# Gate weights rewritten with one-input VectorE operations, adapter casts moved to ScalarE, and the stages put in a new order, in a fused RWKV6 attention and adapter-mixture kernel

## The chip, the cores and the metric

The kernel runs on one core of a Trainium2 chip. The metric is device time in microseconds (us), the median of several executions. Each execution is called fast or slow by its time against the fastest of the same kernel, and only fast runs enter a ratio. The engines are TensorE (PE in the profile, with its weight loads as PEld), VectorE (DVE), ScalarE (ACT), GpSimd (POOL) and SyncE (SP, which here only issues transfers). In these traces each engine takes its instructions in the order in which the program gives them (GpSimd stands 16.1 us at one cast, below), and the kernel fixes that order by hand. SBUF and PSUM are the two memories in which the kernel keeps its tiles: TensorE's products go to PSUM, and nearly everything else lies in SBUF.

## The reference

Two computations follow each other. The first is a recurrence with a decay for each channel (4 batches, 8 heads, 768 steps, 48 channels a head), the second a mixture of low-rank adapters on its output (3072 rows of 384, 8 adapters of rank 16, the best two for each row):

```python
for t in range(S):                                   # S = 768
    cur = einsum('bhd,bhe->bhde', u[None] * kt, vt)
    y[:, :, t] = einsum('bhd,bhde->bhe', rt, state + cur)
    state = wt[:, :, :, None] * state + einsum('bhd,bhe->bhde', kt, vt)
# x = y, laid out as 3072 rows of 384
logits = x @ w_gate                                  # 8 adapters
topk = the two largest of each row;  w = softmax over these two
out = x + sum over the two of w * (x @ A[e]) @ B[e]
```

## The kernel before

The recurrence is cut into 24 tiles of 128 time steps (6 for each batch). For every tile the kernel multiplies r and k by exponentials of summed logarithms of the decay, takes products on TensorE under a triangular mask, and adds what comes from the state. The step's own term, (sum of r·k·u)·v, is made separately: GpSimd multiplies r·k and then by u, VectorE reduces (`diag`), and GpSimd multiplies v by the result. The gate of the mixture is worked out once for four tiles (at the end for two).

Every stage is a function of the tile number t. It has an offset, and the sorted values of t + offset are the program order. An offset therefore decides what stands before what on every engine.

```python
BATCHES = (4, 4, 4, 4, 4, 2, 2)
OFFSET = dict(load=-12.000, ln=-4.318, rk1=-4.189, rku=-4.068, cs=-2.895, exps=-2.541,
    vcast=-2.385, diag=-2.133, dv=-1.717, mult=-2.159,
    # ... cut ...
    lgmm=1.897, adapters=-6.500, gate=2.015, gate2=2.055, zmm=2.129, zw=2.332, zT=2.344,
    zTev=2.602, dmm=2.746, oev=2.790, store=2.913)

def mult(t):          # VectorE: the "r,k product", 128 x 768, two inputs from SBUF
    nc.vector.tensor_mul(rk2[...], st[t]["rk"][...], st[t]["e2"][...])

def rk1(t):           # GpSimd
    rku_ = wk.tile([L, H, D], F32, name="rku")            # two buffers
    nc.gpsimd.tensor_mul(rku_, st[t]["rk"][:, 0], st[t]["rk"][:, 1])
def rku(t):
    nc.gpsimd.tensor_mul(st[t]["rku"], st[t]["rku"], u_sb)
def diag(t):          # VectorE; frees the buffer rku and releases dv
    nc.vector.tensor_reduce(out=dg, in_=st[t]["rku"], axis=AX.X, op=ALU.add)
def dv(t):            # GpSimd
    nc.gpsimd.tensor_mul(dv_, st[t]["v"], st[t]["diag"].to_broadcast([L, H, D]))

def gate2(t):         # VectorE, n = 4 tiles at once; E = 8
    for i in range(n):
        nc.vector.max(out=top[:, i, :], in_=ge[:, i, :])
    nc.vector.tensor_tensor(out=sel, in0=ge, in1=top[:, :, 1:2].to_broadcast([L, n, E]), op=ALU.is_ge)
    nc.vector.tensor_add(den, top[:, :, 0:1], top[:, :, 1:2])
    nc.vector.reciprocal(out=den, in_=den)
    nc.vector.tensor_mul(sel, sel, ge)
    nc.vector.tensor_mul(g, sel, den.to_broadcast([L, n, E]))
# zmm: TensorE x @ A, in the PSUM buffer tagged "m".  zw: VectorE, z times g ("the weighting").
# zT, zTev: transposed, in "m" again.

D_TAG = {NT - 2: "y_ps", NT - 1: "a_ps"}
def dmm(t):           # TensorE: x + zw @ B, in "m" except for the last two tiles
    d_ps = pp.tile([L, HD], F32, name="d_ps", tag=D_TAG.get(t, "m"))
    # ... cut ...

def adapters(t):      # once, at offset -6.5: behind the early loads, ahead of rk1(0)
    nc.sync.dma_start(out=wg_sb, in_=...)     # and A, in three parts, and B
    nc.gpsimd.tensor_copy(out=wg_bf, in_=wg_sb)
    nc.gpsimd.tensor_copy(out=Aall, in_=Aall_f...)
    nc.gpsimd.tensor_copy(out=Ball, in_=Ball_f)
```

The softmax here doesn't subtract the row's maximum and nothing guards it: scores larger than these inputs give would overflow.

## Time and profile before

The time is 141.54 us (median of four runs, 140.98 to 143.12). The end of VectorE's r,k product is a good milestone, because every tile has one and VectorE is close to full in the middle. The trace gives these:

| milestone, us | before |
|---|---|
| second r,k product ends | 27.04 |
| eighth r,k product ends (the start) | 49.22 |
| then four rounds of four tiles, each with one gate | 17.21, 17.76, 17.78, 17.20 |
| last (24th) r,k product ends | 119.17 |
| from there to the end of the span (the tail) | 20.53 |

The first view is the page of before. After the busy times of the engines come rows of 40 digits. Each digit is the busy share, in tenths, of a fortieth of the span; PEclk is the clock that TensorE was granted. The last line is a group of instructions: operation, count, busy time and mean, then the idle time before it and what ended that.

```profile
span 139.7 us, 3124 instructions
PE 90.2 (65%) x1204; PEld 62.6 (45%) x1204; DVE 104.0 (74%) x177; ACT 88.6 (63%) x161; POOL 82.7 (59%) x91
...
DVE  6120000489999999999999999999999899987220
...
POOL 7000005999999996899907999169991597200000
PEclk9999999999999995999999999959998699986755
...
L416 POOL CAST wg_bf<-wg_sb 128x24 bf16<-128x24 f32 x1 | 0.2, 204 | 16.1 <-DMA wg_sb<-in_moe_w_gate_dram 16.1
```

VectorE's row is 9 from slice 10 to slice 35, but for one 8, so VectorE limits the middle. It is nearly empty before, and so is GpSimd's row. The group says what GpSimd does in that time: it waits 16.1 us for the gate weights, which it is to cast.

The second view is that of the waits: who waited, for what, total us, times, longest.

```profile
DVE diag L244 <- POOL rku L240: 17.1, 2, 16.2
...
POOL wg_bf L416 <- DMA wg_sb<-in_moe_w_gate_dram: 16.1, 1, 16.1
...
POOL rku L236 <- DVE diag L244: 14.6, 4, 4.3
```

VectorE stands 16.2 us for the first r·k·u product, which stands behind the casts in GpSimd's program. The third line is another matter: four times GpSimd is out of work for up to 4.3 us, until a `diag` frees a buffer. The next two views show one such place, first VectorE's timeline (start, duration, line, operation).

```profile
64.88 1.55 DVE L223 TENSOR_TENSOR rk_3_150<-rk_in,e_1019 128x768 bf16<-128x768 f32 x1
66.35 0.54 DVE L244 TENSOR_REDUCE diag<-rku 128x8 f32<-128x384 f32 x1
66.81 0.36 DVE L350 MAX8 top<-ge 128x8 f32<-128x8 f32 x4
67.20 0.92 DVE L352 TENSOR_TENSOR sel<-ge,top 128x32 f32<-128x32 f32 x1
...
68.33 0.87 DVE L356 TENSOR_TENSOR sel<-sel,ge 128x32 f32<-128x32 f32 x1
69.23 0.75 DVE L358 TENSOR_TENSOR g<-sel,den 128x32 f32<-128x32 f32 x1
70.09 0.69 DVE L373 TENSOR_TENSOR zw<-z_ps,g 128x512 bf16<-128x512 f32 x1
```

Here is GpSimd's timeline at the same time. The bracket holds the idle time before an instruction and what ended it.

```profile
67.08 1.00 POOL L236 TENSOR_TENSOR rku<-rk_in 128x384 f32<-128x384 f32 x1
68.16 1.00 POOL L240 TENSOR_TENSOR rku<-rku,u_sb 128x384 f32<-128x384 f32 x1
69.11 0.83 POOL L249 TENSOR_TENSOR dv<-v_in,diag 128x384 f32<-128x384 f32 x1
74.23 1.00 POOL L236 TENSOR_TENSOR rku<-rk_in 128x384 f32<-128x384 f32 x1 [4.30 <-DVE diag L244]
```

Read the two together. `diag` ends just before the gate begins and gives GpSimd three products to run, from 67.08 to 69.94. Nearly all of VectorE's gate falls on these. Three operations have 32 elements and take 0.92, 0.87 and 0.75 us, each ending near the end of a GpSimd product. In before's last full gate, where GpSimd has run out of work, the last two take 0.16 and 0.19 us. The gate takes 3.28 us from its maxima to the weighting (66.81 to 70.09), and then GpSimd has nothing to do for 4.3 us. In this trace the two engines hold each other up: VectorE's r,k product takes 0.95 us alone and 1.55 us beside GpSimd (64.88), and the GpSimd product beside it (`dv`, 65.57) takes 1.54 us in place of 0.83.

The last view is that of windows, for the tail: the stretch, its length, busy time and count of PE, PEld, DVE, ACT and POOL, then granted TensorE clock (1.00 is full), DMA share and GB/s.

```profile
119.17:139.70 20.53, 12.16 (x129) 7.76 (x128) 9.94 (x36) 6.86 (x16) 0.83 (x1) 0.71 0.24 87
```

No engine is full there.

### The profile page before, as it was taken

What the parts mean: (1) busy time and instruction counts of PE and PEld (TensorE: products, weight loads), DVE (VectorE), ACT (ScalarE), POOL (GpSimd) and SP (SyncE); (2) the same over time, 40 slices, a digit from 0 to 9 for tenths busy, and PEclk for the clock granted to TensorE, in tenths of its full rate; (3) what the DMA queues carried; (4) which work ended last, traced back from release to release, by engine and by line L of the source; (5) the groups of instructions that cost most, each with busy time, mean ns of one, the idle gap of its engine ahead of it and who ended that gap; (6) DMA issues with size and microseconds to landing.
All of it is one profiled execution on the core that took longest, in us unless ns stands there. A gap on an engine that the chain in (4) does not pass through costs nothing. (4 is left out here: it accounts for less than half of the span.)

```text
span 139.7 us, 3124 instructions
## 1 busy us (share of the span) xinstructions
PE 90.2 (65%) x1204; PEld 62.6 (45%) x1204; DVE 104.0 (74%) x177; ACT 88.6 (63%) x161; POOL 82.7 (59%) x91
## 2 busy tenths in 40 slices
PE   1362400297776928997559784599864997777570
PEld 0131100254555714774547563386653775656320
DVE  6120000489999999999999999999999899987220
ACT  4045600098798962899939998279992799622521
POOL 7000005999999996899907999169991597200000
PEclk9999999999999995999999999959998699986755
DMA  4799999999999300897918811011110111111314
GB/s 145 183 349 391 342 83 300 380 392 387 382 387 386 132 0 2 191 299 252 347 48 281 280 63 56 0 61 56 61 56 0 56 58 62 61 56 56 113 56 169
DMA packets 17470, 24.39 MB, mean 175 GB/s; under 512 B 4912, under 2 KB 14384, under 8 KB 17456
## 3 DMA queue, kind: packets, MB, share of 16 engines
q1 hardware_dynamic: 17456, 24.20, 52.0%
q8 instruction: 9, 0.15, 0.4%
q14 instruction: 5, 0.04, 0.1%
HBM read 19.48 MB, written 4.72 MB: 173 GB/s over the span
## 5 line engine op out<-in xcount | busy, mean ns | idle before, releaser
L236 POOL TENSOR_TENSOR rku<-rk_in 128x384 f32<-128x384 f32 x24 | 27.5, 1146 | 14.6 <-DVE diag L244 14.6
L263 ACT COPY rkT<-trp 128x1024 bf16<-128x1024 bf16 x24 | 24.8, 1032 | 17.1 <-PE trp L257 17.1
L249 POOL TENSOR_TENSOR dv<-v_in,diag 128x384 f32<-128x384 f32 x24 | 28.5, 1188 | 2.0 <-DVE diag L244 2.0
L278 DVE TENSOR_TENSOR at<-a_ps,at_mask 128x1024 bf16<-128x1024 f32 x24 | 29.1, 1214 | 0.0
L244 DVE TENSOR_REDUCE diag<-rku 128x8 f32<-128x384 f32 x24 | 13.0, 543 | 17.9 <-POOL rku L240 17.1
L240 POOL TENSOR_TENSOR rku<-rku,u_sb 128x384 f32<-128x384 f32 x24 | 24.6, 1024 | 1.9
L404 ACT COPY res<-d_ps 128x384 f32<-128x384 f32 x24 | 12.0, 501 | 19.9 <-PE d_ps L399 15.2
L315 DVE TENSOR_TENSOR xs<-dv,y_ps 128x384 bf16<-128x384 f32 x24 | 13.1, 544 | 1.5 <-PE y_ps L309 1.3
L327 ACT COPY xT<-xT_ps 128x384 bf16<-128x384 bf16 x24 | 12.4, 515 | 2.5 <-PE xT_ps L322 2.4
L231 ACT CAST v_bf<-v_in 128x384 bf16<-128x384 f32 x24 | 13.1, 545 | 0.0
L257 PE MATMUL trp<-ident,rk_1_146 128*128 128x128 bf16 x48 | 4.1, 235 | 12.8 <-DVE rk_1_146 L223 12.7
L200 ACT ACTIVATE logw<-w_in 128x768 f16<-128x768 f32 x11 | 9.4, 855 | 3.5 <-DMA w_in<-in_w_dram 3.5
L383 PE MATMUL zT_ps<-ident,zw 128*128 128x128 bf16 x24 | 2.9, 243 | 12.9 <-DVE zw L373 12.9
L398 PE MATMUL d_ps<-xs,ident 128*128 128x384 bf16 x24 | 8.9, 371 | 3.4 <-DVE zT L390 2.6
L212 PE MATMUL cs_ps<-logw,co_strict 128*128 128x384 f16 x20 | 7.3, 367 | 5.8 <-ACT e_197 L218 3.3
L272 PE MATMUL a_ps<-rkT 48*128 48x128 bf16 x192 | 10.6, 236 | 0.0
L294 ACT CAST S_sb<-s_ps 128x384 bf16<-128x384 f32 x20 | 10.3, 513 | 0.0
L214 PE MATMUL cs_ps<-logw,strict 128*128 128x384 f16 x24 | 8.9, 372 | 1.6 <-ACT logw L197 1.6
L416 POOL CAST wg_bf<-wg_sb 128x24 bf16<-128x24 f32 x1 | 0.2, 204 | 16.1 <-DMA wg_sb<-in_moe_w_gate_dram 16.1
L309 PE MATMUL y_ps<-v_bf,at 128*128 128x48 bf16 x192 | 9.4, 189 | 0.5 <-DVE at L278 0.5
L322 PE MATMUL xT_ps<-ident,xs 128*128 128x128 bf16 x72 | 8.6, 232 | 1.5 <-ACT rkT L263 1.4
L257 PEld LDWEIGHTS <-rk_1_146 128*128 128x128 bf16 x48 | 3.1, 105 | 13.7 <-DVE rk_1_146 L223 13.3
(124 smaller groups left out, 219.9 us busy)
## 6 DMA issues: line engine op xcount, KB each, us to landing
rk_in<-in_rk_dram SPq DMA_DIRECT2D x24, 384.0 KB, 6.6
v_in<-in_v_dram SPq DMA_DIRECT2D x24, 192.0 KB, 6.1
out_dram<-res SPq DMA_DIRECT2D x24, 192.0 KB, 1.9
w_in<-in_w_dram SPq DMA_DIRECT2D x11, 384.0 KB, 6.5
w_in<-in_w_dram SPq DMA_DIRECT2D x2, 192.0 KB, 3.5
u_sb<-in_u_dram SPq DMA_DIRECT2D x1, 192.0 KB, 6.7
Aall_f<-in_moe_A_dram SPq DMA_DIRECT2D x3, 64.0 KB, 4.9
Ball_f<-in_moe_B_dram SPq DMA_DIRECT2D x1, 192.0 KB, 3.7
```

The costliest lines, as they stand in the source:

```text
L231: nc.scalar.copy(out=v_bf, in_=st[t]["v"])
L236: nc.gpsimd.tensor_mul(rku_.rearrange("p h d -> p (h d)"), st[t]["rk"][:, 0], st[t]["rk"][:, 1])
L240: nc.gpsimd.tensor_mul(st[t]["rku"], st[t]["rku"], u_sb)
L244: nc.vector.tensor_reduce(out=dg, in_=st[t]["rku"], axis=AX.X, op=ALU.add)
L249: nc.gpsimd.tensor_mul(dv_, st[t]["v"], st[t]["diag"].to_broadcast([L, H, D]))
L263: nc.scalar.copy(out=rkT, in_=st[t]["trp"])
L272: nc.tensor.matmul(a_ps[:, g, p, :], lhsT=rkT[base:base + D, 1, p, :], rhs=rkT[base:base + D, 0, p, :], start=True, stop=True)
L278: nc.vector.tensor_mul(at, st[t]["a_ps"].rearrange("s g p f -> s (g p) f"), at_mask.to_broadcast([128, H, 128]))
L294: nc.scalar.copy(out=sb, in_=S_acc)
L315: nc.vector.tensor_add(xs, st[t]["dv"].rearrange("p a b -> p (a b)"), st[t]["y_ps"].rearrange("p a b -> p (a b)"))
L327: nc.scalar.copy(out=xT_, in_=st[t]["xT_ps"])
L404: nc.scalar.copy(out=res, in_=st[t]["d_ps"])
```

## The change

The change has four parts. The gate loses its three 32-element two-input operations on VectorE; four `tensor_scalar` (compare, then multiply, with two scalars for each row) and a reduction come in, and GpSimd makes one last 32-element product. The adapter casts go to ScalarE, in the middle of its work. The loads go out in another order. And nearly all offsets are new. The intent is to free the start from the late adapter loads and to keep the gate out of GpSimd's way.

```diff
-    load=-12.000,
+    load_w=-14.300,  load_rk=-12.200,  load_v=-12.100,      (was one stage; u now before v)
-    rk1=-4.189,  rku=-4.068,  diag=-2.133,  dv=-1.717,  mult=-2.159,
+    rk1=-2.324,  rku=-2.092,  diag=-0.953,  dv=-0.189,  mult=-2.543,
-    lgmm=1.897,  gate=2.015,  gate2=2.055,  zmm=2.129,  zw=2.332,
+    lgmm=1.556,  gate=1.745,  gmax=1.849,  gsel=1.921,  zmm=2.027,  zw=2.052,
+    casts=1.179,
     ... the other offsets also change; cut, several of them put on one line here ...

-        nc.vector.tensor_tensor(out=sel, in0=ge, in1=top[:, :, 1:2].to_broadcast([L, n, E]), op=ALU.is_ge)
-        nc.vector.tensor_add(den, top[:, :, 0:1], top[:, :, 1:2])
+        nc.vector.tensor_reduce(out=den, in_=top[:, :, 0:2], axis=AX.X, op=ALU.add)
         nc.vector.reciprocal(out=den, in_=den)
-        nc.vector.tensor_mul(sel, sel, ge)
-        nc.vector.tensor_mul(g, sel, den.to_broadcast([L, n, E]))
+        for i in range(n):
+            nc.vector.tensor_scalar(out=sel[:, i, :], in0=ge[:, i, :], scalar1=top[:, i, 1:2],
+                                    scalar2=den[:, i, :], op0=ALU.is_ge, op1=ALU.mult)
+    def gsel(t):
+        nc.gpsimd.tensor_mul(g, st[t]["sel"], st[t]["ge"])

     def adapters(t):
         ...
-        nc.gpsimd.tensor_copy(out=wg_bf, in_=wg_sb)
-        nc.gpsimd.tensor_copy(out=Aall, in_=Aall_f.rearrange("p a e r -> p a (e r)"))
-        nc.gpsimd.tensor_copy(out=Ball, in_=Ball_f)
+    def casts(t):
+        nc.scalar.copy(out=wg_bf, in_=wg_sb)
+        nc.scalar.copy(out=Aall, in_=Aall_f.rearrange("p a e r -> p a (e r)"))
+        nc.scalar.copy(out=Ball, in_=Ball_f)
```

More of the change, by code (lines that the diff above doesn't have):

```diff
@@ L22 @@
 BATCHES = (4, 4, 4, 4, 4, 2, 2)
-STAGES = ("load", "ln", "cs", "exps", "mult", "vcast", "rk1", "rku", "diag", "dv", "tr", "trev", "amm", "aev",
-          "kv", "sev", "ymm", "xev", "xT", "xTev", "lgmm", "adapters", "gate", "gate2", "zmm", "zw", "zT", "zTev",
+STAGES = ("load_w", "load_rk", "load_v", "ln", "ln1", "cs", "exps", "mult", "vcast", "rk1", "rku", "diag", "dv", "tr", "trev", "amm", "aev",
+          "kv", "sev", "ymm", "xev", "xT", "xTev", "lgmm", "adapters", "casts", "gate", "gmax", "gsel", "zmm", "zw", "zT", "zTev",
           "dmm", "oev", "store")
 OFFSET = dict(
-    load=-12.000,
-    ln=-4.318,
-    rk1=-4.189,
-    rku=-4.068,
-    cs=-2.895,
-    exps=-2.541,
-    vcast=-2.385,
-    diag=-2.133,
-    dv=-1.717,
-    mult=-2.159,
-    tr=-1.719,
-    trev=-1.349,
-    amm=-0.767,
-    aev=-0.334,
-    kv=-1.651,
-    sev=-0.667,
-    ymm=0.203,
-    xev=0.439,
-    xT=1.112,
-    xTev=1.398,
-    lgmm=1.897,
-    adapters=-6.500,
-    gate=2.015,
-    gate2=2.055,
-    zmm=2.129,
-    zw=2.332,
-    zT=2.344,
-    zTev=2.602,
-    dmm=2.746,
-    oev=2.790,
-    store=2.913,
+    load_w=-14.300,
+    load_rk=-12.200,
+    load_v=-12.100,
+    ln=-4.517,
+    ln1=-3.548,
+    rk1=-2.324,
+    rku=-2.092,
+    cs=-3.307,
+    exps=-2.892,
+    vcast=-2.132,
+    diag=-0.953,
+    dv=-0.189,
+    mult=-2.543,
+    tr=-1.890,
+    trev=-1.762,
+    amm=-0.918,
+    aev=-0.628,
+    kv=-1.628,
+    sev=-0.979,
+    ymm=-0.097,
+    xev=0.063,
+    xT=0.823,
+    xTev=0.891,
+    lgmm=1.556,
+    adapters=-6.500,
+    casts=1.179,
+    gate=1.745,
+    gmax=1.849,
+    gsel=1.921,
+    zmm=2.027,
+    zw=2.052,
+    zT=2.119,
+    zTev=2.310,
+    dmm=2.544,
+    oev=2.763,
+    store=2.994,
 )
@@ L78, in plan @@
         for t in range(NTILE):
-            if f in ("gate", "gate2", "zmm", "zw", "zT", "zTev") and t not in gate_at:
+            if f in ("gate", "gmax", "gsel", "zmm", "zw", "zT", "zTev") and t not in gate_at:
                 continue
@@ L82, in plan @@
                 continue
-            if f == "adapters" and t > 0 or f == "ln" and t > 0 and t % 2:
+            if f in ("adapters", "casts") and t > 0 or f in ("ln", "ln1", "load_w") and t % 2:
+                continue
+            if f.startswith("load") and t == 0 or f == "ln1" and t > 0:
                 continue
@@ L125, with load_w, load_rk, load_v @@
     st = {t: {} for t in range(NT)}
-    def load(t):
-        if t % 2 == 0:
-            w_in = io.tile([L, 2, HD], F32, name="w_in", bufs=(AHEAD + 4) // 2)
-            if t == 0:
-                nc.sync.dma_start(out=w_in[:, 0], in_=w[0])
-            else:
-                nc.sync.dma_start(out=w_in, in_=w[t:t + 2].rearrange("c p f -> p c f"))
-            st[t]["w"] = w_in
-            st[t + 1]["w"] = w_in
+    def load_w(t):
+        w_in = io.tile([L, 2, HD], F32, name="w_in", bufs=(AHEAD + 4) // 2)
+        for i in range(2):
+            st[t + i]["w"] = w_in
+        if t == 0:
+            for i in range(2):
+                nc.sync.dma_start(out=w_in[:, i], in_=w[i])
+        else:
+            nc.sync.dma_start(out=w_in, in_=w[t:t + 2].rearrange("c p f -> p c f"))
+    def load_rk(t):
         rk_in = io.tile([L, 2, HD], F32, name="rk_in")
         nc.sync.dma_start(out=rk_in, in_=rk[t])
+        st[t]["rk"] = rk_in
+    def load_v(t):
         v_in = io.tile([L, H, D], F32, name="v_in")
         nc.sync.dma_start(out=v_in.rearrange("p h d -> p (h d)"), in_=v[t])
-        st[t].update(rk=rk_in, v=v_in)
-        if t == 0:
-            nc.sync.dma_start(out=st[0]["w"][:, 1], in_=w[1])
+        st[t]["v"] = v_in
+    u_sb = const.tile([128, H, D], F32)
+    def load_u(t):
+        nc.sync.dma_start(out=u_sb, in_=u.partition_broadcast(128))
     gate_at, _ = batches()
     GMAX = max(BATCHES)
-    order = plan()
-    n_pre = next(i for i, (f, _) in enumerate(order) if f != "load")
-    load(0)
-    u_sb = const.tile([128, H, D], F32)
-    nc.sync.dma_start(out=u_sb, in_=u.partition_broadcast(128))
-    for _, t in order[1:n_pre]:
-        load(t)
+    load_w(0)
+    load_rk(0)
+    load_u(0)
+    load_v(0)
     ident = const.tile([128, 128], BF16)
@@ L197, in ln, with ln1 @@
             nc.scalar.activation(out=logw[:, 0], in_=st[0]["w"][:, 0], func=ACT.Ln)
-            nc.scalar.activation(out=logw[:, 1], in_=st[0]["w"][:, 1], func=ACT.Ln)
         else:
             nc.scalar.activation(out=logw, in_=st[t]["w"], func=ACT.Ln)
-        st[t]["logw"] = logw[:, 0]
-        st[t + 1]["logw"] = logw[:, 1]
+        for i in range(2):
+            st[t + i]["logw"] = logw[:, i]
+    def ln1(t):
+        nc.scalar.activation(out=st[1]["logw"], in_=st[1]["w"][:, 1], func=ACT.Ln)
     def cs(t):
@@ L340, in gate, with gmax @@
         st[t]["ge"] = ge
-    def gate2(t):
+    def gmax(t):
         t0, n = gate_at[t]
         ge = st[t]["ge"]
-        def small(nm, w_):
-            return wk.tile([L, GMAX, w_], F32, name=nm)[:, 0:n, :]
-        top = small("top", E)
+        top = wk.tile([L, GMAX, E], F32, name="top")[:, 0:n, :]
+        den = wk.tile([L, GMAX, 1], F32, name="den")[:, 0:n, :]
+        sel = wk.tile([L, GMAX, E], F32, name="sel")[:, 0:n, :]
         for i in range(n):
             nc.vector.max(out=top[:, i, :], in_=ge[:, i, :])
-        sel = small("sel", E)
-        nc.vector.tensor_tensor(out=sel, in0=ge, in1=top[:, :, 1:2].to_broadcast([L, n, E]), op=ALU.is_ge)
-        den = small("den", 1)
-        nc.vector.tensor_add(den, top[:, :, 0:1], top[:, :, 1:2])
+        nc.vector.tensor_reduce(out=den, in_=top[:, :, 0:2], axis=AX.X, op=ALU.add)
         nc.vector.reciprocal(out=den, in_=den)
-        nc.vector.tensor_mul(sel, sel, ge)
-        g = small("g", E)
-        nc.vector.tensor_mul(g, sel, den.to_broadcast([L, n, E]))
+        for i in range(n):
+            nc.vector.tensor_scalar(out=sel[:, i, :], in0=ge[:, i, :], scalar1=top[:, i, 1:2],
+                                    scalar2=den[:, i, :], op0=ALU.is_ge, op1=ALU.mult)
+        st[t]["sel"] = sel
+    def gsel(t):
+        t0, n = gate_at[t]
+        g = wk.tile([L, GMAX, E], F32, name="g")[:, 0:n, :]
+        nc.gpsimd.tensor_mul(g, st[t]["sel"], st[t]["ge"])
         st[t]["g"] = g
@@ L413, in adapters @@
             nc.sync.dma_start(out=Aall_f[:, j, :, :],
-                                in_=moe_A[:, j * 128:(j + 1) * 128, :].rearrange("e fi r -> fi e r"))
+                              in_=moe_A[:, j * 128:(j + 1) * 128, :].rearrange("e fi r -> fi e r"))
         nc.sync.dma_start(out=Ball_f, in_=moe_B.rearrange("e r d -> (e r) d"))
-        nc.gpsimd.tensor_copy(out=wg_bf, in_=wg_sb)
-        nc.gpsimd.tensor_copy(out=Aall, in_=Aall_f.rearrange("p a e r -> p a (e r)"))
-        nc.gpsimd.tensor_copy(out=Ball, in_=Ball_f)
-    fns = dict(load=load, ln=ln, cs=cs, exps=exps, mult=mult, vcast=vcast, rk1=rk1, rku=rku, diag=diag, dv=dv, tr=tr,
+    def casts(t):
+        nc.scalar.copy(out=wg_bf, in_=wg_sb)
+        nc.scalar.copy(out=Aall, in_=Aall_f.rearrange("p a e r -> p a (e r)"))
+        nc.scalar.copy(out=Ball, in_=Ball_f)
+    fns = dict(load_w=load_w, load_rk=load_rk, load_v=load_v, ln=ln, ln1=ln1, cs=cs, exps=exps, mult=mult, vcast=vcast, rk1=rk1, rku=rku, diag=diag, dv=dv, tr=tr,
                trev=trev, amm=amm, aev=aev, kv=kv, sev=sev, ymm=ymm, xev=xev, xT=xT, xTev=xTev, lgmm=lgmm,
-               adapters=adapters, gate=gate, gate2=gate2, zmm=zmm, zw=zw, zT=zT, zTev=zTev, dmm=dmm, oev=oev,
+               adapters=adapters, casts=casts, gate=gate, gmax=gmax, gsel=gsel, zmm=zmm, zw=zw, zT=zT, zTev=zTev, dmm=dmm, oev=oev,
                store=store)
     with tc.manual_schedule(engines={ENG.PE, ENG.Activation, ENG.DVE, ENG.Pool, ENG.SP}):
-        for f, t in order[n_pre:]:
+        for f, t in plan():
             fns[f](t)
```

## The prediction

> **What bounds the kernel now.** Three stretches.
>
> 1. Start, 0 to 27 us. By the timeline, GpSimd has its masks by 3.3 us and then stands until 19.4 at the cast of the gate weights (page, groups: 16.1 us idle, released by its DMA, behind 17 loads in the queue). The casts of A and B follow to 23.2. Behind them, in order, are the r*k*u products; VectorE waits 16.2 us for the first (view of waits), so its second r,k-times-exp product ends only at 27.0.
> 2. Middle. VectorE is 97% busy (windows, 40 to 100). A tile without a gate takes 3.54 us: GpSimd's three products (1.07 + 0.96 + 0.78) plus 0.72 in which VectorE's r,k-times-exp product shuts them out. That product takes 0.95 us alone, 1.56 beside GpSimd; GpSimd's first product then 1.71 instead of 0.99. [...] With a gate in every fourth, four tiles take 17.77 us (72.74 to 90.51). There, three 128x32 two-input operations cost 0.92, 0.87 and 0.75 us beside GpSimd; the last two take 0.16 and 0.19 in the last full gate, without it. GpSimd then idles 4.3 us.
> 3. Tail, from the last r,k product (ends 119.2) to 139.7: gates, TensorE, ScalarE, stores in turn; GpSimd is done.
>
> **What changes.**
> - Casts leave GpSimd: its products can begin when tile 0's r,k land, near 6 us. I estimate the second r,k product near 13 us instead of 27.0 (tile 1's loads near 11, by the pace of before's loads). Given back: ScalarE does the casts after its fifth Exp, near 20 us, but the adapters' DMAs (4.4 us of issue, 83 GB/s) land near 22 to 24, one 384 KB load later than before; ScalarE stands 2 to 3 us. Net at the eighth tile: -12.9 us (49.2 to 36.3).
> - Gate: out go the three two-input operations; in come one reduction (0.15) and four tensor_scalar of 8 elements [...]; GpSimd gets one 32-element product [...]. [...] But the order leaves GpSimd little to run then, so I expect one block of at most 1 us per gate. No trace yet shows it.
> - rku no longer follows rk1 directly, saving 0.12 us: GpSimd-bound tiles near 3.4.
> - Four tiles then take about 15.6 us (estimate: VectorE sum 13.8, plus 1.8 of exclusion and waits; ScalarE 14.0). Four rounds: -8.7 us.
> - Tail: unchanged within 1 us.
>
> **Prediction.** 141.5 - 12.9 - 8.7 = 119.9 us; range 115.5 to 124. Faster by over 2%: 0.97; within 2%: 0.02; slower: 0.01.
>
> **What would show each step.** GpSimd's r*k products from about 6 us, no 16 us wait; second r,k product near 13; a ScalarE wait of 2 to 3 us on an adapter DMA; rounds of 15.6 us, no 4.3 us GpSimd idle (under 1.5)[...].
>
> **What would make it wrong.** Each tensor_scalar blocked by a GpSimd product (+2 us per gate, 128 us in all); tile 1's loads later than 11 us; the ScalarE stand longer; ScalarE (3.5 us per tile) or a slowed TensorE clock becoming the limit; or better sharing (15.0 per round, 117).

The sum came to 119.9 us (141.5 − 12.9 − 8.7). After's trace has 0.195 us from one `tensor_scalar` to the next, 0.287 us in the record of one, and 0.25 us for GpSimd's product of 32 elements. The cut figure of `tensor_scalar` is inside VectorE's 13.8 us of a round. In before's trace the rest of that sum is about 13.4 us, an estimate from the starts of VectorE's instructions: four times the 2.93 us of the tile from 72.74 to 75.67, and 1.7 for what is left of the gate from 84.58 to 89.38. So about 0.4 us of it stood for the four `tensor_scalar`. The other parts are near numbers of the same trace: ScalarE is busy for 14.18 us from 72.74 to 90.51 (14.0 in the prediction), three r,k products beside GpSimd lose three times 0.61 us (1.8), and the addition that the reduction replaces takes 0.153 us (0.15).

## The result, and the profile after

The time after is 123.03 us (median of four, 122.42 to 123.49), against 141.54 in the same rounds. The ratio is 0.872, with a 95% interval of 0.865 to 0.879. A ratio here is the record's own figure for the fast runs of the same rounds, so it is not quite the ratio of the medians quoted. The medians are of all runs, and some hold a slow one (e1, e5, e7 and e8 one each, e2 two, and before in the two later sets of rounds); the profiles read are of fast runs unless the text says otherwise. Before's own median was 141.3 to 141.9 us in the later comparisons. After itself was not run again there.

| us | before | after | difference | predicted |
|---|---|---|---|---|
| eighth r,k product ends | 49.22 | 35.08 | −14.1 | −12.9 |
| eighth to last | 69.95 | 63.37 | −6.6 | −8.7 |
| last to end of span | 20.53 | 22.75 | +2.2 | 0 (within 1) |
| span | 139.7 | 121.2 | −18.5 | −21.6 |

Each of these is read from one profile. After, e7 and e11 below have the same program up to the tail, and their eighth product ends at 35.08, 35.19 and 36.60 us, so a single difference of 1 us is not to be leaned on. After's rounds are 15.67, 15.67, 16.35 and 15.68 us. The page of after has these rows:

```profile
span 121.2 us, 3161 instructions
PE 88.6 (73%) x1204; PEld 62.1 (51%) x1204; DVE 97.8 (81%) x180; ACT 89.9 (74%) x164; POOL 81.5 (67%) x95
...
DVE  6350799866999999999999999999999999862200
...
POOL 7045999986588599965999658696969973200000
PEclk9999999985999999999999967999999997555555
```

GpSimd works from the third slice on and VectorE, at 6 tenths or more until the tail, from the fifth. In the last seven slices the clock is at 5 in six. The waits of after:

```profile
POOL g L375 <- DVE sel L368: 11.1, 6, 5.2
...
POOL rku L250 <- DVE diag L258: 9.5, 7, 1.4
...
POOL rku L250 <- DMA rk_in<-in_rk_dram: 5.3, 2, 4.0
```

The 16 us wait for the gate weights is gone; what GpSimd waits for first is tile 0's own r and k, for 4.0 us. The wait for `diag` is 1.4 us at most, where it was 4.3. The largest wait, for the gate's `sel`, holds mostly time in the tail, where GpSimd has little else to do (5.2 us the longest). ScalarE's timeline shows the casts in their new place:

```profile
21.20 0.22 ACT L435 CAST wg_bf<-wg_sb 128x24 bf16<-128x24 f32 x1
21.76 0.51 ACT L436 CAST Aall<-Aall_f 128x384 bf16<-128x384 f32 x1 [0.33 <-DMA Aall_f<-in_moe_A_dram]
22.77 0.51 ACT L437 CAST Ball<-Ball_f 128x384 bf16<-128x384 f32 x1 [0.51 <-DMA Ball_f<-in_moe_B_dram]
```

ScalarE stands 0.33 + 0.51 = 0.84 us for the transfers. Next are the timelines at a gate, of VectorE and then of GpSimd:

```profile
64.98 1.44 DVE L237 TENSOR_TENSOR rk_3_126<-rk_in,e_1348 128x768 bf16<-128x768 f32 x1
66.34 0.36 DVE L364 MAX8 top<-ge 128x8 f32<-128x8 f32 x4
66.74 0.16 DVE L365 TENSOR_REDUCE den<-top 128x4 f32<-128x8 f32 x1
...
67.15 0.87 DVE L368 TENSOR_SCALAR sel<-ge,top,den 128x8 f32<-128x8 f32 x4
67.93 0.54 DVE L258 TENSOR_REDUCE diag<-rku 128x8 f32<-128x384 f32 x1
68.45 0.69 DVE L390 TENSOR_TENSOR zw<-z_ps,g 128x512 bf16<-128x512 f32 x1
```

```profile
65.56 1.72 POOL L254 TENSOR_TENSOR rku<-rku,u_sb 128x384 f32<-128x384 f32 x1
68.17 0.25 POOL L375 TENSOR_TENSOR g<-sel,ge 128x32 f32<-128x32 f32 x1 [0.88 <-DVE sel L368]
68.55 1.00 POOL L250 TENSOR_TENSOR rku<-rk_in 128x384 f32<-128x384 f32 x1
```

From the maxima to the weighting now takes 2.11 us (66.34 to 68.45), and a `diag` is in it. But note what GpSimd does from 67.29 to 68.17: nothing. It ran out of work 0.13 us after the start of the first `tensor_scalar`: next in its order is the gate's own product `g`, which needs the results of all four, and behind that a product whose buffer the `diag` after the fourth sets free. So the trace of after cannot say whether these operations escape GpSimd, or whether GpSimd was simply not there. In the tail the window of after reads:

```profile
98.45:121.20 22.75, 12.50 (x101) 7.37 (x97) 10.68 (x35) 6.16 (x14) 3.20 (x6) 0.57 0.20 73
```

The clock is 0.57 against 0.71, and the tail is 2.2 us longer. VectorE's timeline shows where the time goes in, counted from the last r,k product: the last product under the mask starts at 6.17 us (5.87 in before), the last gate's maxima at 12.69 (11.79), the last weighting at 15.39 (13.65). So the delay grows step by step, 0.3, 0.9, 1.7 and at the end 2.2 us. Just before that weighting VectorE waits 1.56 us for TensorE's z product, where before it waited 0.86.

### The profile page after: what moved, and what is told of

Its sections match the earlier page's. It is cut to its first block, busy times and chain, and to the rows that moved or that the text cites. A ratio compares the mean times of both kernels' runs of the same rounds, so it can differ in the third digit from the quotient of the medians.

```text
span 121.2 us, 3161 instructions
## 1 busy us (share of the span) xinstructions
PE 88.6 (73%) x1204; PEld 62.1 (51%) x1204; DVE 97.8 (81%) x180; ACT 89.9 (74%) x164; POOL 81.5 (67%) x95
## 4 chain that ended last, share of the span: by engine, by line
DVE 33%; DMA 22%; ACT 15%; PE 13%; issue 9%; SPq 5%; DVEq 0%; ACTq 0%; POOLq 0%
DMA v_in<-in_v_dram 15%; DVE at L292 6%; DVE rk_3_126 L237 5%; DMA rk_in<-in_rk_dram 4%; ACT rkT L277 4%; SPq L430 3%; DVE diag L258 3%; DVE sel L368 3%; DVE xs L329 3%; ACT res L421 3%; DVE rk_2_124 L237 3%; PE d_ps L415 3%; DVE zw L390 3%; DMA Ball_f<-in_moe_B_dram 2%; PE d_ps L416 2%
## 5 line engine op out<-in xcount | busy, mean ns | idle before, releaser
L254 POOL TENSOR_TENSOR rku<-rku,u_sb 128x384 f32<-128x384 f32 x24 | 35.6, 1485 | 0.5 <-DMA u_sb<-in_u_dram 0.5
L250 POOL TENSOR_TENSOR rku<-rk_in 128x384 f32<-128x384 f32 x24 | 23.9, 996 | 15.4 <-DVE diag L258 9.5
L263 POOL TENSOR_TENSOR dv<-v_in,diag 128x384 f32<-128x384 f32 x24 | 19.9, 827 | 2.5 <-DVE diag L258 2.4
L336 PEld LDWEIGHTS <-xs 128*128 128x128 bf16 x72 | 6.3, 104 | 7.1 <-issue 4.9
L375 POOL TENSOR_TENSOR g<-sel,ge 128x32 f32<-128x32 f32 (+1 forms) x7 | 1.7, 242 | 12.0 <-DVE sel L368 11.1
L416 PE MATMUL d_ps<-Ball,zT 128*128 128x384 bf16 x24 | 9.4, 392 | 0.0
L228 PE MATMUL cs_ps<-logw,n_incl 128*128 128x384 f16 x24 | 8.8, 368 | 0.0
```

Source lines behind the costliest of these rows:

```text
L228: nc.tensor.matmul(o, lhsT=wb, rhs=lw, start=False, stop=True, skip_group_check=True)
L250: nc.gpsimd.tensor_mul(rku_.rearrange("p h d -> p (h d)"), st[t]["rk"][:, 0], st[t]["rk"][:, 1])
L336: nc.tensor.transpose(xT_ps[:, j, :], st[t]["xs"][:, j * 128:(j + 1) * 128], ident)
```

## The experiments

Twelve kernels ran, and all gave correct results. The questions were these. Is the start a matter of the casts alone? Is the gain of the middle due to the new gate operations (the theory of the prediction) or to the gate's new place ahead of `diag` (the rival)? And where do the 2.2 us of the tail come from?

### Casts alone, gate operations alone, both

`e1_casts` is before with the casts on ScalarE, behind the fifth exponential:

```diff
+    casts=1.465,
-        nc.gpsimd.tensor_copy(out=wg_bf, in_=wg_sb)       (and the two others)
+    def casts(t):
+        nc.scalar.copy(out=wg_bf, in_=wg_sb)              (and the two others)
```

> The kernel before, with one part of the change: the three adapter casts go from GpSimd to ScalarE, after its fifth Exp, as in the changed kernel. Theory 'queue order': GpSimd's products stood only behind the casts, so they begin near 7 us, the second r,k product ends near 13 to 14 us instead of 27.0, rounds of four tiles stay near 17.5 us, and the time is 128 to 130 us. Rival 'loads': tile 1 is held by its own loads or by TensorE, so less than half of that comes, 135 us or more.

Measured: 130.31 us against 141.9 (ratio 0.919, 0.911 to 0.927), just above the 128 to 130 expected. The second r,k product ends at 13.97 and the eighth at 34.5, both within 1 us of after's. The casts alone are therefore worth 11.6 us of the time. At the eighth tile they bring 14.7 us, but the middle then takes 71.9 us in place of 69.95, and the tail 21.53 in place of 20.53, which gives 2.9 of it back. Its rounds are 17.39 to 18.46 us; why the middle became longer was not tested.

`e2_gate` is before with only the gate's operations replaced, in the old place:

```diff
-    gate2=2.055,
+    gmax=2.055,
+    gsel=2.056,       (with gmax and gsel as in the kernel after)
```

> The kernel before, with only the gate's new operations (reduction, four tensor_scalar, product on GpSimd), at the old place in the order, where GpSimd is busy. Theory 'no blocking': the four tensor_scalar take about 0.9 us as in the changed kernel, each 0.28 to 0.29 us in the record, each gate saves 1 to 1.5 us, time 134 to 137 us. Rival [...]: tensor_scalar is shut out by GpSimd's products too; single ones take up to 1 us, four take over 1.5 us, and the time is 138 us or more.

Measured: 144.85 us, ratio 1.010 (1.001 to 1.020): no gain, at most a small loss. Its profiled run was a slow one, so no reading of its trace is used here. Two of its four runs were slow ones too; the ratio uses the other two (143.1 and 144.35).

`e3_casts_gate` is the two together.

```diff
  e1_casts, and:
-    gate2=2.055,
+    gmax=2.055,
+    gsel=2.056,
```

> The kernel before with both parts, casts and gate operations, but the old order of stages and loads. What is left to the changed kernel (123.0 us) is the worth of the reordering. Theory 'the operations do it': 122.5 to 124.5 us, the reordering is worth under 1.5 us. Rival 'the order does it': 126 us or more.

Measured: 131.06 us, ratio 0.920 (0.914 to 0.928); e1 had 0.919 without the new operations. In the old place, the new operations bring nothing. VectorE's timeline of e3 at a gate, and GpSimd's, say why:

```profile
72.87 1.76 DVE L356 TENSOR_SCALAR sel<-ge,top,den 128x8 f32<-128x8 f32 x4
...
75.06 0.69 DVE L378 TENSOR_TENSOR zw<-z_ps,g 128x512 bf16<-128x512 f32 x1 [0.43 <-POOL g L363]
```

```profile
72.33 1.00 POOL L238 TENSOR_TENSOR rku<-rk_in 128x384 f32<-128x384 f32 x1
73.41 0.99 POOL L242 TENSOR_TENSOR rku<-rku,u_sb 128x384 f32<-128x384 f32 x1
```

The four `tensor_scalar` take 1.76 us beside a busy GpSimd, and 0.87 in after. The view of lines gives, for one instruction, the shortest, median and longest duration in ns; first e3, then after:

```profile
L356 DVE TENSOR_SCALAR sel<-ge,top,den x24: 278/288/1037, 36.4 to 121.3; 128x8 f32<-128x8 f32 x24
```

```profile
L368 DVE TENSOR_SCALAR sel<-ge,top,den x24: 284/286/292, 35.8 to 112.0; 128x8 f32<-128x8 f32 x24
```

A `tensor_scalar` has one tensor input and still is shut out, for up to 1037 ns. How the block comes about, no trace shows. In after all 24 stay within 8 ns of each other, so the order had removed what they could collide with.

### The old gate operations in the new order

`e4_after_oldgate` is after with the three two-input operations put back:

```diff
-    gmax=1.849,
-    gsel=1.921,
+    gate2=1.849,      (with gate2 as in the kernel before)
```

> The changed kernel with the old gate operations (three two-input VectorE operations) at the new place in the order, where GpSimd has nearly run out of work. Theory 'operation type': each of the three is again shut out by GpSimd, rounds go from 15.7 to over 17 us, time 128 us or more. Rival 'place': with GpSimd idle they cost 0.15 to 0.2 us each, with at most one block, and the time is 122 to 124.5 us, as without the new operations.

Measured: 121.0 us, ratio 0.850 (0.843 to 0.857), against 0.872 for after. This is a little below even the range of 'place'. The old operations are not slower in the new order; they are faster, by about 2 us between the medians, which stem from different rounds. The rounds are 15.58, 16.27, 15.58 and 16.26, in sum 63.69 against 63.37, so the middle is the same. The mean durations of the three operations, in the five gates of four tiles, are 590, 160 and 193 ns; before they were 718, 715 and 640. The difference between e4 and after lies in the tail: 20.72 us against 22.75.

### The new place alone

`e9_gate_first` is e1 with three offsets changed, and nothing else. The gate then stands ahead of `diag`.

```diff
-    lgmm=1.897,
+    lgmm=1.800,
-    gate=2.015,
-    gate2=2.055,
+    gate=1.850,
+    gate2=1.860,
```

> e1 (130.3 us) with three offsets changed and no operation: logits, Exp and gate come earlier, so that VectorE does the gate before, not after, the reduction that gives GpSimd its next product; everything else in the old order. Theory 'place': GpSimd runs out of work just when the gate runs, the three two-input operations fall from 0.92, 0.87 and 0.75 us to 0.15 to 0.6, rounds fall from 17.5 to 15.5 to 16.3 us, time 122 to 125.5 us. Rival 'the whole new order is needed': rounds stay above 17, 128 us or more.

Measured: 121.91 us, ratio 0.864 (0.857 to 0.870). Three numbers take 130.3 to 121.9 us, with the old two-input operations and the old order of the rest. The rounds are 16.89, 16.03, 16.05 and 15.43 us, in sum 64.40 against e1's 71.87; the first is longer than expected. The gain is in the tile with the gate: from the second round on it takes 5.5 to 5.6 us from one r,k product to the next, and 7.3 in before, while the other three tiles of the second and of the third round add up to 10.5 us in both. TensorE's clock does not explain it: e9's two middle rounds and before's second have it at 1.00 throughout, and take 16.03, 16.05 and 17.76 us. VectorE's timeline of e9, and the line of GpSimd that follows:

```profile
67.66 0.42 DVE L353 TENSOR_TENSOR sel<-ge,top 128x32 f32<-128x32 f32 x1
...
68.28 0.16 DVE L357 TENSOR_TENSOR sel<-sel,ge 128x32 f32<-128x32 f32 x1
68.48 0.19 DVE L359 TENSOR_TENSOR g<-sel,den 128x32 f32<-128x32 f32 x1
```

```profile
69.21 1.00 POOL L237 TENSOR_TENSOR rku<-rk_in 128x384 f32<-128x384 f32 x1 [1.18 <-DVE diag L245]
```

The first of the three meets the end of a GpSimd product that was already running, and the other two run at the speed of an idle neighbour. The gate takes 1.78 us from maxima to weighting with a `diag` in it; in e1 it took 3.28 without one. GpSimd's idle time of 4.3 us at a gate becomes 1.18 us here and 1.35 us at the next tile.

`e10_pool_late` reaches the same relation from the other side. It leaves the gate where e1 has it and moves GpSimd's chain later:

```diff
-    rk1=-4.189,  rku=-4.068,  diag=-2.133,  dv=-1.717,
+    rk1=-2.270,  rku=-2.040,  diag=-0.900,  dv=-0.140,
```

> e1 (130.3 us) with the four offsets of GpSimd's chain moved as in the changed kernel (both products later, the reduction one tile later and after the gate, the third product between the first two); gate, TensorE and ScalarE stages in the old order. Theory 'place': same as the run with the gate first, 121 to 125 us, rounds 15.5 to 16.3; and single tiles bound by GpSimd at 3.42 instead of 3.54. Rival: 128 us or more.

Measured: 122.19 us, ratio 0.865 (0.858 to 0.872), with rounds of 16.25, 15.58, 15.58 and 16.27 us. It does what e9 does, and tiles that GpSimd holds up take 3.42 us, as expected. The five kernels with the casts on ScalarE make a table of operations by place:

| gate's place | old two-input operations | new operations |
|---|---|---|
| behind a `diag` | e1: 130.31 us | e3: 131.06 us |
| ahead of a `diag` | e9: 121.91; e4: 121.0 | after: 123.03 |

With the old operations the place alone is worth 8 us (e9, e10), and the whole new order 9 (e4). With the new operations only the whole order was tried, and it is worth 8 (e3 to after). The operations are worth nothing in the old place and cost about 2 us in the new order (e4 against after, which differ in nothing else).

### The casts back on GpSimd, and the loads back in their old order

`e5_after_oldcasts` is after with the casts on GpSimd again:

```diff
-    casts=1.179,
-        nc.scalar.copy(out=wg_bf, in_=wg_sb)              (and the two others)
+        nc.gpsimd.tensor_copy(out=wg_bf, in_=wg_sb)       (inside adapters)
```

> The changed kernel (123.0 us) with the three casts back on GpSimd, issued with the adapter loads as before. Theory 'queue order': GpSimd's products stand behind the casts again, the second r,k product goes from 13.1 us to about 25 to 27, and the time rises by 10 to 13 us, to 133 to 136. Rival: the new order of the chain on GpSimd (products later) makes it less sensitive, under 5 us.

Measured: 134.22 us (132.96 to 135.77), ratio 0.950 (0.943 to 0.957). The time is 11.2 us above after's, so the casts are worth nearly the same from both sides. One part was missed: the second r,k product does not go back to 27 us but stays at 13.6, because the new order has it ahead of the first `diag`. The wait moves on: GpSimd waits 17.4 us for the gate weights, the first `diag` waits 12.0 us for GpSimd, and the eighth r,k product ends at 46.5. The profiled run was a slow one, so these four numbers tell which wait there is, not its exact size.

`e6_after_oldloads` is after with before's order of loads:

```diff
-    load_w=-14.300,  load_rk=-12.200,  load_v=-12.100,
+    load_w=-12.003,  load_rk=-12.002,  load_v=-12.001,    (and at first w0, rk0, v0, w1, u)
```

> The changed kernel (123.0 us) with the loads in the old order. Theory 'loads do little': within 1.0 us of it, 122.2 to 124 us; the second r,k product within 1 us of 13.1. Rival: w loaded earlier is what fills the start, 124.5 us or more.

Measured: 123.25 us, ratio 0.875 (0.870 to 0.881), against 0.872. The order of the loads makes no difference in time that these runs resolve. The second r,k product ends at 14.26 us, just outside the 1 us expected, and the eighth at 35.91.

### The tail

`e7_tail_dve` is after with the last two gate products on VectorE. It tests whether the hop to GpSimd lengthens the tail.

```diff
-        nc.gpsimd.tensor_mul(g, st[t]["sel"], st[t]["ge"])
+        eng = nc.vector if t >= NTILE - 4 else nc.gpsimd
+        eng.tensor_mul(g, st[t]["sel"], st[t]["ge"])
```

> The changed kernel (123.0 us), but the product of the last two gates on VectorE instead of GpSimd. It asks where its longer tail (22.8 us from the last r,k product against 20.5 before) comes from. Theory 'hop to GpSimd': each of the two gates loses 0.3 to 0.45 us, so 122.2 to 122.7 us, and the tail falls by 0.3 to 0.9. Rival 'TensorE clock': it was halved through the whole tail (granted clock 0.57 and 0.50), the hop is nearly all hidden: 122.8 us or more unless the clock happens to differ.

Measured: 122.91 us, ratio 0.872 (0.865 to 0.880), the same as after. The tail is 22.06 us, 0.7 shorter, which would fit the theory; but the profiled run is the fastest of its four (121.83 us), and the tail of e6, where the hop is still in, is shorter yet. So the hop is not what makes the tail 2 us longer. These are the tails of e4 and of e6:

```profile
99.18:119.90 20.72, 11.30 (x106) 6.64 (x105) 10.14 (x37) 6.40 (x15) 2.51 (x3) 0.68 0.24 86
```

```profile
99.32:121.10 21.78, 11.02 (x101) 6.50 (x97) 10.60 (x35) 6.15 (x14) 3.21 (x6) 0.68 0.21 76
```

The tail of e6 has after's program, instruction for instruction, but the clock is at 0.68 where after had 0.57.

`e11_fill` keeps TensorE busy in the tail with products that nobody reads, to see what the low clock costs:

```diff
+    def fill(k):
+        for _ in range(k):
+            nc.tensor.matmul(cs_ps[:, 0, 0:HD], lhsT=ones, rhs=cpos, start=True, stop=True,
+                             skip_group_check=True)
+    (12 before zT(19), 5 before zT(21), 4 before zT(23), 3 before zmm(23),
+     and 2 each before dmm of tiles 16, 18, 19, 20, 21)
```

> The changed kernel (123.0 us) with idle matmuls of 128x384 put on TensorE, in its waits, in the tail (result unused, PSUM bank free by then). Theory 'clock': the halved TensorE clock costs the tail 1 to 2 us; with fillers the granted clock stays at 1 for most of the tail, and the tail (22.8 us) falls to 21 to 21.8, time 121 to 122.2 us. Rival 'the tail hangs on the chain of waits, not on TensorE': same or longer than 123 us, even where the clock is full.

Measured: 120.98 us (six runs, 120.43 to 122.18), ratio 0.860 (0.854 to 0.864). The window of its tail:

```profile
99.99:120.50 20.51, 13.79 (x135) 7.97 (x131) 10.59 (x35) 6.06 (x14) 3.22 (x6) 1.00 0.23 81
```

The clock is at 1.00, and the tail is 20.51 us against 22.75, although TensorE has 34 products more to do in it. The time falls by 2.05 us. Twelve of the 34 stand where TensorE idles longest in after's tail, 2.10 us (99.12 to 101.22) before the first transposition of weighted z; in this tail after's clock is at full until there, and at half from then to the end (1.00 from 98.45 to 101.22, then 0.51 on average). From 101.7 to 116.0 us after's clock is 0.50; e11's is 1.00 over its whole tail. What lowers the clock was not shown: up to its last product TensorE's longest idle time is 2.10 us in after's tail and only 0.88 us in before's, yet before's clock was at 0.50 too, from 124.7 to 127.2 us.

`e8_oldgate_tags` is e4 with two more tiles' last products in PSUM banks of their own, so that the last z product need not wait until ScalarE has copied them out of the shared one:

```diff
-    D_TAG = {NT - 2: "y_ps", NT - 1: "a_ps"}
+    D_TAG = {NT - 5: "a_ps", NT - 4: "y_ps", NT - 2: "y_ps", NT - 1: "a_ps"}
```

> A try for a faster kernel: e4 (121.0 us) with two more of the last output products (tiles 19 and 20) in PSUM banks that are free by then, so the last gate's z product needn't wait for three output copies in turn through one bank. Theory 'one bank in the tail': the z product of the last gate begins about 2 us earlier after the last xs, time 118.5 to 119.7 us. Rival: the tail hangs on the logits of the last tile, time 120.3 us or more.

Measured: 118.88 us (117.96 to 119.77), ratio 0.839 (0.832 to 0.846), the fastest of all. Its tail:

```profile
99.01:117.60 18.59, 9.00 (x101) 5.82 (x97) 10.14 (x36) 5.86 (x14) 2.51 (x3) 0.89 0.25 89
```

It is 2.1 us shorter than e4's, and the clock is 0.89 against e4's 0.68. The last weighting starts 12.30 us after the last r,k product, in e4 13.82, and no longer waits for the z product (1.64 us in e4). The shorter waits and the higher clock come together; how much each brings was not separated.

`e12_first_tags` puts the pieces on before: the casts, e9's three offsets and these two banks.

```diff
  e9_gate_first, and:
+    D_TAG = {NT - 5: "a_ps", NT - 4: "y_ps", NT - 2: "y_ps", NT - 1: "a_ps"}
```

> A try for the smallest change that beats both: the kernel before, with the casts moved, the gate ahead of GpSimd's reduction (three offsets) and two more output products in free PSUM banks. Expected 119 to 120.5 us: the run with the gate first (121.9) less the 2 us that the banks gave e8. Rival: the banks help only the new order, 121.5 us or more.

Measured: 120.92 us (120.05 to 121.69), ratio 0.859 (0.853 to 0.864). This is just above what was expected. Its tail is 19.02 us, as hoped; what it lacks against e8 is in its first rounds, 16.92 and 16.73 us where e8 has 15.21 and 16.25. So a few edits to before do more than the whole change did, and e8 shows that the rest of the new order is worth some 2 us more.

## Why the prediction was right or wrong

The time came out at 123.03 us, inside the range of 115.5 to 124 and 3.1 above the 119.9 predicted. The direction was right. The three terms of the sum missed by −1.2, +2.1 and +2.2 us, which add up to the 3.1.

1. **The start: right, a little undervalued.** It was to be −12.9 us and was −14.1. The mechanism, casts that block the products behind them in GpSimd's queue, is shown by e1 and, from the other side, by e5. The term that was mis-sized is ScalarE's stand at the casts: 2 to 3 us in the prediction, 0.84 us in the trace. That this makes up the 1.2 us was not tested, and e11, with the same start, reached its eighth tile only at 36.60. The second r,k product came at 13.15, as estimated ("near 13").

2. **The middle: the size near, the reason wrong.** The step that failed is "Gate: out go the three two-input operations", as the source of the gain in a round. e3 makes exactly this exchange in the old place and gains nothing; e4 takes it back in the new place and loses nothing. What the rounds gained, e9 and e10 gain by the place alone (64.4 and 63.7 us for the four, after 63.4). That the size came near was luck as far as the operations go: the order that came with them brought it. The prediction had the decisive remark, "the order leaves GpSimd little to run then", but used it only to argue that the new operations would not be blocked. The same remark holds for the old ones. And it missed that a gate behind `diag` costs twice: VectorE runs it while GpSimd has its three products, and GpSimd then stands 4.3 us because the next `diag` is late.

3. **The size of the middle: 6.6 us in place of 8.7.** Two terms were off. The prediction took 17.77 us for all four rounds of before, but the first and the last are 17.21 and 17.20, which is 1.1 us. And one round of after took 16.35 in place of 15.6, about 0.7 us. TensorE's clock dips in that stretch of the page; that this is the reason was not tested, but other traces point the same way. In after, e4, e6, e7, e10 and e11 the clock is 0.89 or 0.90 in all eight rounds of 15.79 us or more, and 1.00 in the sixteen others, of 15.58 to 15.70.

4. **The small operations, "one block of at most 1 us per gate": none in after.** There the `tensor_scalar` start 0.195 us apart (four in 0.78 us, 67.15 to 67.93) and none is longer; one record is 0.286 us. Before's trace has VectorE's small operations at 0.15 to 0.19 us when nothing blocks them, and e9 has two of the gate's two-input ones at 0.16 and 0.19, so four of the one-input kind are not cheaper than two of these. The block that was feared, up to 1 us, is real and shows in e3 (1037 ns), where GpSimd is busy. The one-input form is no shield.

5. **The tail: wrong.** It was to be "unchanged within 1 us" and was +2.2. The tail was counted in instructions; TensorE's clock, which fell from 0.71 to 0.57, and the wait for the last z product were left out. With the clock held at 1.00 (e11) the time falls by 2.05 us. That is not the share of the fall from 0.71 to 0.57: before's tail takes 20.53 us at 0.71, and after's needs a clock of 1.00 for 20.51. The tail of e6 helps to split the 2.2 us, by single profiles and so roughly. With after's program at a clock of 0.68 it takes 21.78, so about 1 us goes with the clock. Up to the last gate's maxima e6 is as early as before (11.76 us after the last r,k product, before 11.79), but its weighting then waits 1.56 us for the z product where before waited 0.86. With the new order this wait is 1.28 to 1.64 us (e4, e6, e7), with the old one 0.86 to 1.19; at e11's full clock it is 0.94, and with two more PSUM banks it is gone (e8, e12). The chain of the new gate is longer as well (in the first of the last two gates, 1.54 us from maxima to weighting, 1.10 in before), but taking GpSimd's product out of it (e7) gave back 0.09 us of that and no time. Why the clock falls further in after than in e6 and e4, and what makes up the rest, stays open.

6. **The other signs held.** GpSimd's products begin at 7.3 us, the 16 us wait is gone, and its idle time at a gate is 0.88 us and 1.35 us at the next tile (predicted under 1.5). Tiles that GpSimd holds up take 3.42 us (predicted 3.4, before 3.54).

## What to carry to other kernels

When two engines hold each other up, as VectorE's r,k product and GpSimd's `dv` do here (0.95 and 0.83 us alone, 1.55 and 1.54 together), first ask which instruction gives the other engine its next work, and put the small operations ahead of it: three offsets brought 8.4 us here, where rewriting the same operations brought nothing. In an engine that runs in program order, as GpSimd does here (16.1 us at one cast), an instruction that waits for a late transfer holds up everything behind it, so put it where its data have landed. And when a tail is a chain of small steps, look at TensorE's granted clock (held at 1.00 in e11, 2.05 us less) and at shared PSUM banks (two more in e8, 2.1 us less in the tail, with a higher clock as well) before counting instructions.
